# A new written-out plan for a fused attention and mixture-of-experts kernel, with the last results kept in k's buffer and the last narrow store on two queues

## The chip, the cores and the metric

The kernel runs on one core of a Trainium2 chip: TensorE (PE, with its weight loads PEld shown apart), VectorE (DVE), ScalarE (ACT), GpSimd (POOL), and SyncE (SP), which here only issues DMAs. ACT and POOL can issue DMAs too. The metric is the device time of one execution in microseconds (us). The median of 13 runs of the kernel before is 226.5 us, from 225.05 to 229.55.

## The reference

Two layers in a row, for a batch B of 8, 8 heads, a sequence S of 576 and a head size of 64 (a model width D of 512), with 4 experts of width 64, of which each token uses two:

```python
def _attn_ref(q, k, v, g_norm):
    kv = np.einsum('bhsd,bhse->bhde', k, v)
    out = np.einsum('bhsd,bhde->bhse', q, kv)
    rms = np.sqrt(np.mean(out * out, axis=-1, keepdims=True) + 1e-06)
    return (out / rms * g_norm).astype(np.float32)

def _moe_ref(x, w_gate, wq, wk, wv, wo):
    logits = x @ w_gate
    ...
    for e in range(E):
        q = x @ wq[e]; k = x @ wk[e]; v = x @ wv[e]
        scores = scale * (q @ k.transpose(0, 2, 1))
        ...
        ye = a @ v @ wo[e]
        ...
```

The first layer is linear attention without a mask, normalized over each head. In the second, `w` is the softmax over the two best logits of a token, `a` the softmax of the masked scores, and `ye` is added with its `w` where the expert was chosen. The first layer's output, with the heads side by side, is the x of the second layer, which is causal attention inside each expert.

## The kernel before

The sequence is cut into five blocks of tokens, four of 128 and one of 64 (numbers 0 to 4; block 4 is the narrow one). The two layers run batch by batch. For a batch b the steps, with the short names that the plan uses, are:

- Loads: `lk`, `lv` (k and v, in four parts for batch 0 and two for the others), `lkr`, `lvr` (the last 64 tokens of k and v, two DMAs each), `lq` (q; five blocks of two DMAs for batches 0 and 1, eight pieces for the others). The weights come by `lw` and `lwo`, with `ws` (POOL or DVE) and `wo` (ACT) to scale or convert them.
- `kv` 0 to 3: the products of k and v on PE, two heads each, all in one PSUM bank. `kvc` copies them to the tile kvx (line 420). `kgm` and `kgr` multiply them with the gate's weights and sum (lines 425 and 432, DVE); `kgx` copies those sums into kvx as well. For batch 0 these four steps are split in two halves, the second of which needs kv 2.
- `q`, `qc`: q transposed on PE and copied (batches 0 and 1), or transposed by DVE (the rest).
- `out` 0 to 4: q times kvx (line 466); `oc` copies a block to the tile o_sb; `sq`, `red` square and sum it (lines 492 to 502); `ln`, `rs` and the four small steps `na` to `nd` make the reciprocal root; `gl`, `lg` the gate's logits.
- `xm` scales a block (line 557, POOL), `x` transposes it on PE, `xc` copies it to xT.
- `m8`, `sh`, `ex`, `md`, `mk`, `gt`, `den`, `rd`, `gate`: the gate, on [128 x 20] tiles.
- `v`, `qp`, `kp`: the projections on PE, with copies `vc`, `qpc`, `kpc` (tiles vext, qTp, kT).
- `sc`, `exp`, `msk`: scores in four pieces for each of two pairs of experts (line 672, PE; line 686, ACT; line 692, POOL). `pv` (line 706): the products with v in two groups of blocks, 0 to 2 and 3 to 4. `rc`, `iv`, `oc2` (lines 723, 727, 734) divide by the row sums and multiply with the gate. `ot`, `otc` transpose and copy the result to OT.
- `y` (line 764, PE), `yc` (the copy to SBUF, line 771) and `st` (the store, line 777). The narrow block's result lies as two halves of 64 partitions and 256 columns, so its store is two DMAs.

What runs on which engine is not found by a scheduler when the kernel is built: it is written out in four constants. `ORDER` lists all 1291 steps, two characters for each; every engine works through its own in that order. `ENGINE` has a letter for each step that can run on more than one engine: A for ACT, V for DVE, G for POOL. `SLOTS` gives the buffer or PSUM slot that each tile takes when it is first used. `ZEROS` puts matmuls of a zero tile, whose results nothing reads, ahead of some steps of PE.

PSUM is held as four pairs of two banks. The code tracks for each bank which engine used it last; an instruction of another engine on the same bank waits for that one (`own_waits`), also if both only read. So two engines that read one bank take turns.

All loads but batch 0's v are issued on SP's queue, and all stores. Batch 0's `lvr` and `lv` go by ACT's queue. Small loads of the norm's and the gate's weights go by POOL's, at the start. In the built program every load or store on SP's and ACT's queues waits for the one eight before it, counted over both queues in the plan's order.

The results `y` have four SBUF buffers, y0 to y3, in turn; a copy into one waits until the store that last read it is done.

Of the kernel before, what the change touches and what calls it, by code (L numbers as in the profile page):

```python
# [24 lines left out]
ORDER = (
    "090E010403080507020u060H0v003F0D0c0A0F0G3C0b0J0I0d0C0a0j0i0B0e0f0k390s0g3H0l0m0h0t381A0n163B1C1B1D0w3718170o19"
    "0y3A0x1Q0q1R0p0z1S1T3Y0U1U0r0+1V3Z3E1k1E1F1G12100-1H5f1h1I111l143U1m3G1J131Y151i3V3D1K1j1Z1L1M3L1a0S1N1O3K5g0V"
    "3I1P1W3S5l1b1X0K1n3J3T0Q1e3W3M3N0M3Q5i1q1o1r1p3X0T1c5e3O1f1s201g3P225c213q1d0L1+233r3R5d3e0R1-1t3a0N3f1u5b3g3i"  # L30
    "1v3b3h3m3c0W3s3d2W3j5j3t3n243k2X0O3o3l2UAS3p253u1y2V1w5h1z3v3w2e1x3x5r3y2f5m3z2b460X2Y2h885s2c4C5p2i2Z5k0P5q40"
    "4D5t5uAV474E4926485v8C43418D274A5w423+4S4B2d5n3-2E2g4T2H284F2F442a864I4U4G2I4J4H5y2G452B5o292k4V4K2j4L5x4Q2J2C"
    "2A2l802m4M2n4N4a2o4R2D2p2q2r2L0Y4b2KAR2P4Y2M2Q2N2R2O4y4Z854l4z4c4m814i4d4n4f5z4+5+4j844e5-4g4k4-89630Z4h836059"
    "6450615A535156826B6562575B6766525487586C6F68552SAa6D6G2s4O2T2t4W6H8A6E692x4X6A344P2yAZ316I4p35324o2z6J4t8H6K4u"
    "4q4v6L364r8G6M4s6N8N8F6O6d338E8MAX4w8I6X2+4x8B8J6e2-5D6U6f6Y308K2u6R6ZAW6V5H2v6t8L5I6a6W5J6S2w6u5CAT6T6P6r5E5F"
    "6Q6b6s6p6g6cCt6x5G6j6h6q6k6v6i6y8P6l7N6w6m8O7P7OCz6n8UAc6o7QAe8Y8VAU8W7a8Z7X7b7R7Y8Q7c8XAd7S7Z7U8R8g8a7TAY5K7V"
    "8b6-8hAb8S7W8c5L8i708TC-7d8d8j7e8e6z7fCs7i7j8f7gAi6+7hCxAh8k7k8l7A8m77Ao8n7BC+748o7C7871An8pAgCy8yAq72AfAp92Cv"
    "5Y758zAk8-7l5Z93Aj8+5V5a948v5PAl905QFU8q9I915W5R8s8wAm9J9K5X8x7m73Av8r769LCw7995AzAw9896D199977DAx9A8t9BCuA+7F"
    "Ay7GAr8uA-7H9C9QAs9DD0B0AtB59RFM7EAuB17ID3B67J9q7KHjB7DD9OB8B2HkD59rB3D69PD7HiB49bDC9YB99c9VBA9Z9d9SD2D4BB9T9a"
    "9ED8FHBC9oD99WBD9UBE9G9FBFFQDABT9M7L5M7M9HFJBN5S9p5NBU5T9N7wBQBGBV9-5UDB9s7xA09vBK9tBW9y7yDE7q9wBXBOBZDF5OBHBL"  # L40
    "BPBRHlBMBaA1DK9XBS9u9zBj9xDLHm9eBk9+9f7r9gDOFLBYDM9jA2BbDP7sA39k9hFODNBlDQBIFRA7A4BmBc9lDSA8DRA5BJFIBdA9BpBeDT"
    "A69iBnBqFKBhBoCFBiHnDGCGDWFTDHCDDXHqDIDJDYBfHuCEDUDZAA9mBg7nAB9nCQFPDVCNCRCK7oCSCOCHFXFNCICPFW7pFYCLCJFVFSDaCM"
    "ALDbFZDcCTDdFaAMHoCUDeACDfCYDlAFFbANAD7tAGBrDgAECVFcCWDhCZDiCaAHHyCXBsHxHr7uDoHzFeDuC07vDxBwC1FgBzBxHvBtDyFdD+"
    "HwDrB+FfDvHtD-AIH+ByBuFlB-DwAJHpDzC2FtE0H-BvAKC3FuE1FmC4HsFpI0FnFhFqE2FoE3FrFxI1C8C5C9FiC6FsAOFy7zFjAPDsCA7+AQ"
    "C7CbFzDpDtFkCBCc7-DmI3FvDqEAF+CCDjFwE8DkCgF-E9CpG0DnChCmI2CqCiG1EgCnG2I4CrG3G4I5CdG5EhCoEGEBG7CeG6CfGMCjGAEHI6"
    "CkGPGNIAClGQI7GOGJEEIBI8IMEFICECINI9ERGREDGDELIDESEOGSEMEIGTE6IOEJGKGUIEIPGGGLEPEeEKENIFEQE7IIEfIGETE4IHIJErE5"
    "ElIKEsEiEmEoEVEtILEjEUEnEZGEEaEWEbIQEXGBEpEkEYGHEcGFEqG8GIGCGZEdIRG9GbISGaITGXIUGcIVGdGYIWGVIbIXGfGeInIYGWH3Gg"
    "IqIoIrIpIkEvH4EuEzH5IsEwE+ItExE-IeEyIlH6IuF0IvIcImIhF1HGIdH7HHHAH8HIHDFEHEF5H9FFIyFGF6HBHFF8IzFBF9F7HCF2FCIiFA"
    "IZFDIjIfIaGhIgF3IwGiJ0F4IxGsJ1GpGtGjGqGuGmJWGkGrJ6GnJXGlJYGoJ7I+JZJ2I-J4J3GwJ5GvG+HKG-GxH0GyJHGzJaJIHJHOJbJJJj"
    "HPHLJgHQHMJkHNJcJhJBJlJEHRJCJiH1J8HSH2JFJDJdHfJ9JGHWHgHcHhJeJAHZHdJLHaJfHeJKHXJPJmJQHbJMJRJnJNJoHYJOJpJUHTJqJS"  # L50
    "JVJrJuJTJsHUJvJtHVJ-K2K0JwJyJxK1K3K8K4JzK5J+K6K7K9KA"
)
ENGINE = (
    "VAVAVAVAVAVVVVVVVVVVVGVVVVVGVGVVVAVAVVVVAVVVVVVVVAVAVAVAVAVVAVVVAVVAAVVVAVVAAVAAAGAGAAGGAGAAGGAGGVGVVGVVGVVGVV"
    "GVVVGAGGGVVGVVVVVVVVVVVVVVVAGVAGVAGVAGVVVGVVGVVVVAVVVAGVAGVAGVAGVVVGVVGVVAVAVVAVVAVVAVVVVVVVVVVVVVVVVVVVAVVAVV"
    "VAVAVVVVVAAVVAAVVAAVVAAVVAAVAAGGGGGVGVAGVAGVAGVAGVAVGAGGGVVGVAVAVVVVVAVAVVVAGVAGVAGVAGVVVGVVGVVAVVVVVAGVAGVAGV"
    "AGVVVGVVGVVVVAVVAVVAVVVVVAVVVVVVVVVVVVVVVVVVVAVVAVVVVVAGVVVGVVAAVVVGVVAGVAAGGGGGVGVAGVAGVAGVAGVAVGAGGGVVGVVVVV"
    "AVVVAVAVAVAGVAGVAGVAGVVVGVVGVVAVVVVVAGVAGVAGVAGVVVGVVGVVVVVVVAVVAVVVVVAVVVVVVVVVVVVVVVVVVVVVVVVVVVVVAVVAGVVVAV"
    "VAGVVVGVAAGGAGGVGVAGVAGVVGVAGVAVGAGGGVVGVVVVVVVVVVVVVVVAGVAGVAGVAGVVVGVVGVVAVVVVVAGVAGVAGVAGVVVGVVGVVVVAVVAVVV"
    "VVAVVVVVVVVVVVVVVVVVVVVVVAVVAVVVVVVGVVAAVVAGVVVAVVVAVAAAGGGGVGVAGVAGVAGVAGVAVGAGGGVVGVAVAVAVAVAVVVVVAGVAGVAGVA"  # L60
    "GVVVGVVGVVAVAVVVAGVAGVAGVAGVVVGVVGVVAVAVVAVVAVVAVVAVVVVVVVVVVVVVVVVVVVVVVAVVVVVAAVVVGVVVGVVAGVVVAVAAAGAGGVGVVG"
    "VVGVAGVAGVVVGAGGGVVGVVVAVAVVVAVVVVVAGVAGVAGVAGVVVGVVGVVVVVVAVAGVAGVAGVAGVVVGVVGVVVVVVVVVVVVVVVVVVVVVVVVVVVVVVV"
    "VVVVVVVVAVVVVVAGVVVGVVAAVVAGVVAGVAAAGAGGVGVVGVAGVAGVVGVAVGAGGGVVGVVVAVAVVVVVAVAVAGVAGVAGVAGVVVGVVGVVVVVVAVAGVA"
    "GVAGVAGVVVGVVGVVVVAVVAVVAVVVVVVVVVVVVVVVVVVVVVVVVVVVVVVVVVVVGVVAGVVAAVVAGVVAGVAAGGGGGVGVVGVVGVVGVVGVVVGAGGGVVG"
    "VAVVVVVAVVVAVAVAGVAGVAGVAGVVVGVVGVVVVVVVVAVAGVAGVAGVAGVVVGVVGVVVVAVAVVAVVVVVAVVVV"
)
# [52 lines left out]
def kernel(  # L119
# [161 lines left out]
    def copy(task, dst, src):  # L281
        if engine[task] == "A":
            nc.scalar.copy(dst, src)  # L283
        else:
            nc.vector.tensor_copy(out=dst, in_=src)  # L285
# [580 lines left out]
```

The softmax here doesn't subtract the row's maximum and nothing guards it: scores larger than these inputs give would overflow.

## Time and profile before

The profiled execution took 226.79 us; its span, from the first instruction to the last, is 225.08 us, and 1.71 us lie around it.

| Where | What | us |
| --- | --- | --- |
| runs | median of 13 | 226.5 |
| profile | the execution / its span | 226.79 / 225.08 |
| page, 1 | ACT, POOL busy | 133.3, 125.7 |
| order of time | first zero matmul on PE | 1.25 |
| order of time | first `kv` product of batch 0 | 9.92 |
| order of time | first `out` | 18.05 |
| order of time | first `x` | 26.32 |
| order of time | first `v` projection | 35.35 |
| order of time | last `exp` ends | 214.6 |
| order of time | last y copy ends | 221.43 |
| order of time | last store's issue ends | 222.7 |

A row in order of time begins with its start and length, then the engine, the line and operation, the tiles written and read, the form, and in brackets how long the engine had been idle before it and what ended that. The granted clock is that of TensorE, as a share of its full rate. The zero matmuls all lie in the first 14.4 us.

The transfers of the first 125 us keep the 16 DMA engines nearly full; from 158 us on only stores are left. The page's row of it, in tenths for 40 slices:

```profile
DMA  4978979998999987988799999897334000040065
```

### The profile page before, as it was taken

How to read it: one execution, taken by the hardware profiler on the slowest of the kernel's cores; microseconds unless marked ns; L12 is line 12 of the kernel's file. 1: busy time of each engine (PE TensorE's matmuls, PEld its weight loads, DVE VectorE, ACT ScalarE, POOL GpSimd, SP SyncE). 2: the span in 40 equal slices, each digit the busy share in tenths (PEclk: the TensorE clock that was granted, in tenths of full speed). 3: DMA queues.
4: the chain of work that ended last, by engine and by line, in shares of the span. 5: the costliest groups of instructions: out<-in, count | busy, mean ns of one | idle time of the engine just before them, and what ended most of it. 6: DMA issues, size and time to landing. Idle time of an engine off the chain costs nothing. (4 is left out here: it accounts for less than half of the span.)

```text
span 225.1 us, 6608 instructions
## 1 busy us (share of the span) xinstructions
PE 210.5 (94%) x2550; PEld 179.1 (80%) x2562; DVE 157.5 (70%) x366; ACT 133.3 (59%) x265; POOL 125.7 (56%) x278
## 2 busy tenths in 40 slices
...
DMA  4978979998999987988799999897334000040065
GB/s 130 316 223 263 299 183 231 342 230 112 163 326 236 152 191 236 205 164 183 180 229 301 288 231 256 144 227 138 73 106 155 3 0 4 23 186 3 0 216 210
DMA packets 92576, 40.29 MB, mean 179 GB/s; under 512 B 66688, under 2 KB 88192, under 8 KB 92544
## 3 DMA queue, kind: packets, MB, share of 16 engines
...
q0 software_dynamic: 128, 0.01, 0.0%
...
## 5 line engine op out<-in xcount | busy, mean ns | idle before, releaser
L686 ACT ACTIVATE PT<-p 128x1024 bf16<-128x1024 f32 (+1 forms) x64 | 50.3, 841 | 6.6 <-PE p L672 6.1
L692 POOL TENSOR_SCALAR_AFFINE_SELECT PT<-PT 128x256 bf16<-128x256 bf16 (+1 forms) x80 | 29.1, 382 | 26.4 <-ACT PT L686 25.8
L557 POOL TENSOR_TENSOR x_tok<-o_sb,rstd 128x512 fp32r<-128x512 f32 x40 | 43.0, 1130 | 0.5
L466 PE MATMUL p<-kvx,qT 128*128 128x136 f32 (+1 forms) x320 | 39.2, 285 | 1.1 <-DVE kvx L285 0.7
L466 PEld LDWEIGHTS p<-kvx,qT 128*128 128x128 f32 (+1 forms) x320 | 34.7, 179 | 3.9 <-DVE kvx L285 0.9
L502 DVE TENSOR_REDUCE ms<-sq 128x8 f32<-128x520 f32 (+1 forms) x40 | 26.9, 684 | 7.3 <-POOL sq L498 3.6
L498 POOL TENSOR_TENSOR sq<-o_sb 128x512 f32<-128x512 f32 (+1 forms) x20 | 20.6, 1038 | 12.7 <-DVE ms L502 6.4
L626 PE MATMUL p<-wv_r,xT 128*128 128x256 f32 x160 | 25.6, 295 | 0.7 <-ACT xT L283 0.7
L567 PE MATMUL p<-ident_r,x_tok 128*128 128x128 f32 (+1 forms) x160 | 23.4, 279 | 0.7 <-DVE vext L285 0.3
L567 PEld LDWEIGHTS p<-ident_r,x_tok 128*128 128x128 f32 x160 | 20.6, 191 | 3.8 <-POOL x_tok L557 1.0
L672 PE MATMUL p<-qTp,kT 64*128 64x64 f32 (+4 forms) x192 | 22.0, 343 | 1.3 <-DVE kT L285 0.5
L283 ACT COPY o_sb<-p 128x544 f32<-128x544 f32 (+1 forms) x29 | 15.1, 532 | 13.0 <-PE p L466 12.5
L626 PEld LDWEIGHTS p<-wv_r,xT 128*128 128x128 f32 x160 | 21.2, 192 | 1.9 <-ACT xT L283 0.8
L645 PE MATMUL p<-xT,wk_r 128*128 128x288 f32 x128 | 21.0, 307 | 0.0
L405 PE MATMUL p<-v_b,k_b 128*64 128x64 f32 x512 | 20.1, 224 | 0.0
L764 PE MATMUL p<-wo_b,OT 128*128 128x512 bf16 (+1 forms) x85 | 18.2, 343 | 1.7 <-issue 0.5
L645 PE MATMUL p<-xT,wq_r 128*128 128x288 f32 x128 | 19.8, 300 | 0.0
L405 PEld LDWEIGHTS p<-v_b,k_b 128*64 128x64 f32 x512 | 17.8, 138 | 2.3 <-issue 1.9
L672 PEld LDWEIGHTS p<-qTp,kT 64*128 64x128 f32 x192 | 14.2, 185 | 6.4 <-ACT PT L686 1.5
L645 PEld LDWEIGHTS p<-xT,wk_r 128*128 128x128 f32 x128 | 17.8, 190 | 1.5 <-DVE xT L285 0.5
L285 DVE COPY o_sb<-p 128x544 f32<-128x544 f32 (+1 forms) x19 | 12.0, 629 | 9.5 <-PE p L466 4.2
L706 PEld LDWEIGHTS <-PT 128*128 128x128 bf16 x480 | 16.6, 99 | 2.4 <-POOL PT L692 0.5
(111 smaller groups left out, 348.0 us busy)
## 6 DMA issues: line engine op xcount, KB each, us to landing
...
```

Source lines behind the costliest of these rows:

```text
L405: nc.tensor.matmul(p_kv[hh * Dh : (hh + 1) * Dh, c, :], lhsT=lhs, rhs=rhs, start=(j == 0), stop=(j == NF), skip_group_check=True,)
L466: nc.tensor.matmul(p_o[p0 : p0 + nt, c // 2, c % 2 * 256 : c % 2 * 256 + 2 * GW], lhsT=qTs[b % NQT][:, c * S + i * P : c * S + i * P + nt] ...
L498: nc.gpsimd.tensor_tensor(out=dst, in0=src, in1=src, op=AluOpType.mult)
L502: nc.vector.tensor_reduce(mss[b % 2][:nt, i, :], sqs[(NB * b + i) % 3][:nt], axis=AX_X, op=AluOpType.add)
L557: nc.gpsimd.tensor_tensor(out=buf(("x", b, i), [P, NCH, P], FP32R, "x_tok")[:].rearrange("p c (h r) -> p h r c", h=H), in0=ob[:, i, :, 0:D ...
L567: nc.tensor.matmul(p_t[:, c * P : c * P + nt], lhsT=tiles["x", b, i][:, c, :], rhs=ident_r[:, 0:nt], start=True, stop=True)
L626: nc.tensor.matmul(p_v[:, 0 : E * Hd], lhsT=blocks_of(xTs[b % 2], c)[:, i * P : (i + 1) * P], rhs=w_r["v"][:, c, :, :].rearrange("p e f -> ...
L645: nc.tensor.matmul(p_p[:, s, 0:HALF], lhsT=w_r[nm][:, c, 2 * pr : 2 * pr + 2, :].rearrange("p e f -> p (e f)"), rhs=blocks_of(xTs[b % 2], ...
L672: nc.tensor.matmul(p_s[:, el, o : o + hi - lo], lhsT=kTs[(2 * b + pr) % 3][pp, kb * P : (kb + 1) * P], rhs=tiles["qTp", b, pr][pp, lo:hi], ...
L686: nc.scalar.activation(PT[:, :, d0 : d0 + o], big("sc", b, pr, j)[:, :, 0:o], ACTF.Exp, scale=scale)
L692: nc.gpsimd.affine_select(out=d, in_=d, compare_op=AluOpType.is_ge, fill=0.0, base=0, pattern=[[0, 2], [1, w]], channel_multiplier=-1,)
L764: nc.tensor.matmul(p_y[o * nq : (o + 1) * nq, 0:w], lhsT=lhs, rhs=wo_b[:, pr, o * w : (o + 1) * w], start=(pr == 0), stop=(pr == EP - 1), ...
```

## The change

Three things change; nothing of what is computed does.

1. `ORDER`, `ENGINE`, `SLOTS` and `ZEROS` are new. 163 of the steps that can run on either of two engines move to the other one: ACT now has 14 of the 16 kT copies (6 before), 30 of the 40 xT copies (24), 30 of the 40 o_sb copies (24), 22 of the 40 vext copies (17) and 19 of the 40 y copies (25). The zero matmuls become 22 ahead of `gb` (the gate weights' products, now PE's first real step), 3 ahead of q(0,0) and 1 ahead of out(0,4): 26 in place of 22.

PE's order for batch 0, before and after (numbers in brackets: batch and block, or batch and part):

```
before  q(0,4) gb kv(0,2) gr kv(0,1) kv(0,3) kv(0,0) q(0,3) q(0,0) out(0,4) out(0,3) out(0,0)
        q(0,1) q(0,2) q(1,4) out(0,1) out(0,2) x(0,4) q(1,2) x(0,3) x(0,0) kv(1,3) kv(1,2) kv(1,0) ...
after   gb gr q(0,2) kv(0,3) kv(0,1) kv(0,0) q(0,3) q(0,4) kv(0,2) q(0,0) out(0,4) out(0,3) out(0,0)
        out(0,2) q(0,1) q(1,0) q(1,3) out(0,1) q(1,4) q(1,1) x(0,3) x(0,4) x(0,0) v(0,3) v(0,0) v(0,4)
        kv(1,3) kv(1,2) kv(1,0) kv(1,1) x(0,2) x(0,1) q(1,2) ...
```

The loads and stores in their order, the start:

```
before  lvr(0) lq(0,4) lv(0,0) lk(0,2) lv(0,1) lkr(0) lv(0,2) lv(0,3) lk(0,1) lk(0,3) lk(0,0) lq(1,2)
        lq(0,3) lq(0,0) lvr(1) lq(0,2) lq(0,1) lk(1,1) lq(1,4) lv(1,0) lkr(1) lk(1,0) lv(1,1) lw(v,1) ...
after   lvr(0) lk(0,1) lk(0,3) lv(0,0) lq(0,2) lv(0,1) lv(0,2) lv(0,3) lkr(0) lk(0,0) lq(0,3) lq(0,4)
        lk(0,2) lw(q,1) lvr(1) lq(0,0) lv(1,1) lq(1,0) lq(1,1) lq(0,1) lq(1,3) lv(1,0) lw(v,0) lq(1,4)
        lk(1,0) lw(v,1) lk(1,1) lkr(1) ...
```

The `ws` of the first q weights is now POOL's first step of the plan, ahead of two of its memsets. At the end, PE's order differs in a few places, `yc` of blocks 1 and 2 of batch 6 go from ACT to DVE, and in batch 7 ACT gets blocks 0 (of batch 6), 1 and 4, DVE blocks 2, 0 and 3.

2. The last batch's results of blocks 0 to 3 go to one tile in a slot of k's buffers, so they share no buffer with earlier stores.

3. The second half of the last batch's narrow block is stored by ACT's queue; the first half stays on SP's. The last store on SP is now block 3.

```diff
-ZEROS = {("q", 0, 4): 8, ("gb",): 2, ("kv", 0, 2): 6, ("kv", 0, 1): 3, ("q", 0, 3): 3}
+ZEROS = {
+    ("gb",): 22, ("q", 0, 0): 3, ("out", 0, 4): 1,
+}
...
+    def y_t(b, qc):
+        if b == B - 1 and qc < NF:
+            return buf(("k", "y"), [P, NF, D], FP32, "k_b")[:, qc]
+        return buf(("y", b, qc), [P, D], FP32, "y")[:]
+
     def y_copy(b, qc):
         w = D * blocks[qc][1] // P
-        copy(("yc", b, qc), buf(("y", b, qc), [P, D], FP32, "y")[:, 0:w], small("y", b, qc)[:, 0:w])
+        copy(("yc", b, qc), y_t(b, qc)[:, 0:w], small("y", b, qc)[:, 0:w])
 
     def store(b, qc):
         s0, nq = blocks[qc]
         for o in range(P // nq):
             w = D * nq // P
-            nc.sync.dma_start(out[b, s0 : s0 + nq, o * w : (o + 1) * w], tiles["y", b, qc][o * nq : (o + 1) * nq, 0:w])
+            eng = nc.scalar if b == B - 1 and o else nc.sync
+            eng.dma_start(out[b, s0 : s0 + nq, o * w : (o + 1) * w], y_t(b, qc)[o * nq : (o + 1) * nq, 0:w])
```

More of the change, by code (lines that the diff above doesn't have):

```diff
@@ L20 @@
 PARTS = (((0, 1), (1, 3), (3, 5)), ((0, 5),), ((0, 5),), ((0, 5),), ((0, 5),), ((0, 5),), ((0, 5),), ((0, 5),))
-ZEROS = {("q", 0, 4): 8, ("gb",): 2, ("kv", 0, 2): 6, ("kv", 0, 1): 3, ("q", 0, 3): 3}
+ZEROS = {
+    ("gb",): 22, ("q", 0, 0): 3, ("out", 0, 4): 1,
+}
 ORDER = (
[L28 to L51, printed above, removed]
@@ new lines @@
+    "090206010C03050708000H0D0E040M0F3C0q0G0J0d0A0r0I0b0a3A3D0s0f0e0u0g3E0c0N0v0h0j0B0i0k0m3G0t0n0l381A160S1C1B3H1D"
+    "0w181237190y171Q0o1R0U140z1S15393Q1T1E1F1U0x1G3W1V3R1H0p1k1I133B3X0+1J0T5g3Y1h103S0-3Z5c111Y1i3T1K3F1l1L1j0V1Z"
+    "1m1M0O201a1N1O5f1P1w211W221b1x1X0K3L231n0Q3K1e5l3I1q3J1o5e1r1p1f1s3M1t1u1c1v3N1g3U1d5d0P2U3O5b260R2V3P3V3q270L"
+    "3e873r3a5j3f3g3i5o3b3h3m3c3j893k2W3s3d3n5i3l243o2X3t5h5r3p255n2e3u3v2E3w2b2f3x0W5q3y862F2g5s2H3z5p2c8B4C2Y5u2I"
+    "1y465k2Z281z2B5t405m5v2h294D47490Y4E2i2C415w48801+430X4A1-424S3+4B442G3-824T4O4F452A4U4I4P4G4J4a4H5y2d4V4K842D"
@@ new lines @@
+    "4L5x2a4Y2j4b2JAT0Z2L4M5z4N4Z2l2P5+8D2Q4l4c4m2p2K2R4d2q4n882r5-2M2N4e2O638A604i61812k64624f4j2m4y2n2o65AX4k4g4+"
+    "66AS4z4h6B4-6F6CAd596G506D5A53518556676H6E57835B2S6I522s684Q582T542t4WAV694R2x8N4X348C552y6A4p2z356J4o4t6K8M31"
+    "4u6L362+6M4q326N4r2u6O2-5D4v6dAR4s5C5H4w6X5E336e4x8H6f305F6U5G8G8F8P6R8E8O2v6Y5ICt8J6a6V2w6Z6S6P6WAU8I6b6T8K6t"
+    "6c6r6u6p5JAc6s8L6v6Q6q6g8U6wC+6j6h6k6i8Y8V6lCw6m6n8W8Q6o8Z8XAY7N8aAb8R8b7P8S7OAW5K8T7Q8gD25L6-Aa8h8i7aD3707X7R"
+    "7b7Y7U8j7cCy8c7S7ZCz6z8d7T7V8eAZAi6+Ah7W8fAe7A778k7B748lFH787C71Ag7279Af5YCx8mAk75736x8n8o5V5ZC-8p6y5PAj76Al5M"
@@ new lines @@
+    "8y5W5a7D5Q7EAo5N925X8z7F7I5R7eAmAq8+8-935O7iAp7d94D08v9I7fAn909J8q5SD1918s8w8rAv958xCv7j5T967k988t7gAw997h7G9K"
+    "7J8u7HAz5U977KAx9A9L9QCu9BAyA+9CA-9DAr9RB0CsB5AsB1B6AtAuB7FQ7lB29qDD7mB3FTB89E9rDE9OFM9FB49o9PFLDFB9DCBA9bBB9Y"
+    "FJ9cBC9V9p9d9ZD5FUD69W9a9-FOD7BDA09XBE9sA1HqBF9v9tD4BTBGBWHp9y9wD9BN9SBU9THi9GBXDABZBQBOBVD89MBPDB7LBaHjBH9H9N"
+    "BR9z7MBjBKDOBSBkHnBYBl9UDPBbDK9uBcBmFIDQ9xBd9+9eDRDLBLBe9gHrA2DM9h9iA3BMDN9fFKA77qA4A89jA5A97w9k7rA6DS7x9l7sBI"
+    "DTBh7yBJDGBiHkBpDHDIBnHmBqDJCFBoDUFNCDCGHtDVFWCEHlFXCQCNCRCKCSCOFRCHFVCICPFYFPDWCLFaCJAAFSBfDXCM9mFbABHv7nBrFZ"
@@ new lines @@
+    "DY9nHuBgFcALDZBsCTHo7oAMCUDaCVC0DbCWCYBz7pDcC1CXBwCZB+DdCaBtC2FeANDeHyDfBuB-FdHsHxDlFgBxHzFfHwDgACDiDhH+FlDxAD"
+    "H-DoAEAFFm7tAGDyFpFnDzI0AHFhD+FqDuFoI1FrAOFiD-7zDrAPFxFsFjAQCb7+FyE0DvBvFkFtBy7-DwCcFzE17uC3FuC4I37vFvAIF+DsAJ"
+    "I2DpDtAKDmFwEADqDnDjF-E2EBI4E6E3G0DkG1E8C8I5G2C9G3EgE9G4CAG5C5E7G7G6EGEhGMC6GPI6C7GNEHGQGAGOEEI7GRGJGSGTIAEFI8"
+    "IMIBERGDINELESEOEMI9EIICECEJGKEDGGIEIDGLEPGUCBEKIFIIENCCEQIOEeIGIJIPCgEfIKIHCpChCmCqETCiErILElEsCrCnEiIQEtEmEo"
+    "CdCoCjIREjEnCeE4ISITCfGEEpEkGBCkGHGFEqG8GCIUClGIGZIVG9IWGXE5IbIXGaGdGYGbInGeIYGVGcGfGWIqIoIrIpIkH3GgIsIeItEvIu"
@@ L52 @@
+    "H4EVIhEzEuEZEUEwIlEaExEWEbE+IiEXE-IvH5ImIjEyEYF0H6J0F1EcJ1IcEdHGIdH7HHHAH8HIHDFEHEF5H9FFIyFGF6HBHFF8IzFBF9F7F2"
+    "HCFCIZFAIfIaFDGhIgIwF3GiJWF4IxGsJXGpGtGjGuGqGmJ6GkGrJYGnGlJ7I+GoJZJ2I-J4J3GwJ5GvG+HKG-GxH0GyJHGzJaJIHJHOJbJJJj"
+    "HPHLJgHQHMJkHNJcJhJEJlJBHRJFJiJ8HSH1J9JGJdH2HfJCJAHWHgJeHZJDHhHXHcHaJLJfHYJKHdJmHbJMJPJnJNJoJQHeJOJpHTJqJSJRJu"
+    "JTJrJUHUJsJvJtJVJ-HVK2K0JwJyK3K1JxJzK4K8K5J+K9KAK6K7"
 )
 ENGINE = (
-    "VAVAVAVAVAVVVVVVVVVVVGVVVVVGVGVVVAVAVVVVAVVVVVVVVAVAVAVAVAVVAVVVAVVAAVVVAVVAAVAAAGAGAAGGAGAAGGAGGVGVVGVVGVVGVV"
@@ L55 @@
[L55 to L64, printed above, removed]
@@ L65 @@
-    "VAVVVVVAVVVAVAVAGVAGVAGVAGVVVGVVGVVVVVVVVAVAGVAGVAGVAGVVVGVVGVVVVAVAVVAVVVVVAVVVV"
+    "VAVAVAVAVAVVVVVVVVVVVVVGVVVGVVVVVAVAVVVVVVVVVVVVVAVVVAVVVVVVAVVAAVVVAVVVAVVAAVAAGGAGAAGGGGAAAGAGGVGVAGVAGVAGVA"
+    "GVAVGAGGGVVGVAVVVVVAVAVAVAVAGVAGVAGVAGVVVGVVGVVVVVVAVAGVAGVAGVAGVVVGVVGVVVVAVVAVVAVVVVVVVVVVVVVVVVVVVVVVAVVAVA"
+    "VVVVVAVVVAGVVAAVVAAVVAGVVAGVAAAGAGGVGVAGVAGVVGVAGVVVGAGGGVVGVAVVVAVAVAVAVVVAGVAGVAGVAGVVVGVVGVVVVVVAVAGVAGVAGV"
+    "AGVVVGVVGVVAVAVVAVVAVVAVVAVVVVVVVVVVVVVVVVVVVAVVVVVVVVVAVVAAVVAGVVAGVVVGVAAAGAGGVGVAGVVGVAGVAGVVVGAGGGVVGVAVAV"
@@ new lines @@
+    "AVAVVVVVAVAGVAGVAGVAGVVVGVVGVVVVVVAVAGVAGVAGVAGVVVGVVGVVAVVVVAVVVVVAVVVVVVVVVVVVVVVVVVVVVVAVVVVVVVVAGVVAAVVAAV"
+    "VAGVVAGVAAAGGGGVGVAGVAGVAGVAGVAVGAGGGVVGVVVAVAVVVVVAVAVAGVAGVAGVAGVVVGVVGVVVVVVAVAGVAGVAGVAGVVVGVVGVVAVAVVVVVA"
+    "VVAVVAVVVVVVVVVVVVVVVVVVVAVVVVVVVVAAVVAAVVAAVVAGVVVGVAAGGAGGVGVAGVAGVAGVAGVAVGAGGGVVGVVVVVAVVVVVAVAVAGVAGVAGVA"
+    "GVVVGVVGVVAVAVAVAGVAGVAGVAGVVVGVVGVVVVVVVAVVVVVVVVVVVVVVVVVVVVVVVVVVVVAVVVVVVVVAAVVAAVVAAVVVGVVAAVAAGGGGGVGVAG"
+    "VAGVVGVAGVAVGAGGGVVGVAVVVAVAVVVAVAVAGVAGVAGVAGVVVGVVGVVAVAVAVAGVAGVAGVAGVVVGVVGVVAVAVVVVVVVVVVVVVVVVVVVVVVVVVV"
@@ L66 @@
+    "VVVVVAVVAVVVVVVAVVAGVVAAVVAGVVAGVAAGGAGGVGVAGVVGVAGVAGVAVGAGGGVVGVVVVVAVAVAVVVAVAGVAGVAGVAGVVVGVVGVVVVVVVVAGVA"
+    "GVAGVAGVVVGVVGVVVVAVVVVVVVVVVVVVVVVVVVVVVVVVVVVVVVAVVAVVVVVAGVVAGVVVGVVAGVVVAVAAGGAGGVGVVGVVGVVGVAGVVVGAGGGVVG"
+    "VVVVVAVAVVVAVAVAGVAGVAGVAGVVVGVVGVVAVAVVVAVAGVAGVAGVAGVVVGVVGVVVVVVVVVAVVVVVVVVAV"
 )
 SLOTS = (
-    "00001110101112023002102233201400051233020013433023201032531021332240313130230101330223032101201101312231100321"
-    "03213023001450125330041553671046715124206076504703012002312304131301521310305463730144000161154030511021123100"
@@ L70 @@
-    "21032031300212304020355310033454230511002671100030021301312130131233012011162710120630302105741002011007622113"
-    "76237645370022034133033513001020167021101712013140501230131220522000011345101132110062711036712067201230130130"
-    "0130210201126701672451030121067001267145340621"
+    "00000232113011012116270332430526703203146320720300302012030301231025312211310014153101541100212100310103210301"
+    "01013203145674523304500110411567211261010064576213201304101230122220312345364301124503541254101123010131013010"
@@ L73 @@
+    "03110113202331020033304453205672160132012003120013201023060012017014150230121310111030312120434223335002011320"
+    "12131000530432013231026711062140527312001671456201510014250322401310141501101670120673203617223263130203120110"
+    "1010231201322033230011223301100123023167621"
 )
```

## The prediction

> **What bounds the kernel now.** I read the page's busy shares first, then the stretches (busy time by window), then the first 19 us and the last 8 us in order of time.
>
> ```profile
> PE 210.5 (94%) x2550; PEld 179.1 (80%) x2562; DVE 157.5 (70%) x366; ACT 133.3 (59%) x265; POOL 125.7 (56%) x278
> ```
>
> PE is the bound; no other engine passes 70%. The stretches say where PE is not. Their columns are the stretch, its length, then busy time (and instructions) of PE, PEld, DVE, ACT and POOL, the granted clock, the DMA share and GB/s.
>
> ```profile
> 6.06:18.05 11.99, 9.53 (x137) 6.24 (x137) 5.86 (x19) 2.88 (x6) 1.97 (x10) 1.00 0.92 260
> 18.05:26.32 8.27, 7.09 (x81) 6.36 (x81) 3.77 (x7) 5.37 (x16) 2.29 (x6) 1.00 0.98 289
> 26.32:35.35 9.03, 8.87 (x168) 8.30 (x166) 7.01 (x16) 3.92 (x11) 7.33 (x14) 1.00 0.80 200
> 35.35:53.85 18.50, 18.14 (x205) 16.77 (x204) 13.44 (x23) 12.33 (x26) 9.41 (x14) 1.00 1.08 249
> 53.85:57.26 3.41, 2.49 (x21) 1.88 (x20) 2.50 (x10) 2.86 (x8) 2.92 (x11) 1.00 0.84 145
> 57.26:60.68 3.42, 3.42 (x39) 2.97 (x38) 1.98 (x7) 2.62 (x4) 1.59 (x6) 0.50 1.49 147
> 60.68:208.10 147.42, 144.90 (x1759) 127.81 (x1767) 110.95 (x248) 93.26 (x182) 90.13 (x189) 1.00 0.70 163
> 208.10:225.10 17.00, 11.27 (x140) 6.87 (x140) 7.80 (x23) 9.58 (x15) 4.87 (x17) 0.98 0.40 141
> ```
>
> From 60.68 to 208.10 PE idles 2.52 us in 147.42 (1.7%), from 35.35 to 57.26 it idles 1.28 in 21.91 (5.8%), and 57.26 to 60.68 ran at half clock: 3.42 us for 1.71 us of work. So a new order can win at most 3.8 us of idling plus 1.7 us of clock in the middle; the rest lies in the first 35 us and the last 17.
>
> In the start the load queue and a chain on DVE decide:
>
> ```profile
> 4.82 2.49 SPq L306 DMA_DIRECT2D k_b<-in_k_dram  x3
> 13.66 0.69 DVE L425 TENSOR_TENSOR kvg<-p,wg_t 128x512 f32<-128x512 f32 x1 [0.74 <-PE p L405]
> 15.51 0.69 DVE L425 TENSOR_TENSOR kvg<-p,wg_t 128x512 f32<-128x512 f32 x1 [0.66 <-ACT kvx L283]
> 16.12 1.27 DVE L432 TENSOR_REDUCE kvxg<-kvg 128x8 f32<-128x512 f32 x2
> 17.30 0.69 DVE L285 COPY kvx<-kvxg 64x8 f32<-64x8 f32 x4
> 18.05 2.73 PE L466 MATMUL p<-kvx,qT 128*64 128x136 f32 x24 [0.70 <-DVE kvx L285]
> ```
>
> The first out matmul waits for kvx, the last of a chain behind the four kv products; the second kvg multiply waits for ACT to leave the same bank. That is a turn of readers.
>
> **The start, step by step.** In the program's order every load waits for the one issued eight loads before it; SP, free at 4.23, issues its next k load at 4.82. Landings of before in the first 20 us, issue to landing: k_b 5.2 us (3.7 to 5.6), q_b 4.1 to 4.7, v_b 4.5 to 5.5, v_rem 2.8 to 3.6. One SP issue takes some 0.63 (six q loads in 3.80).
>
> The 22 zero matmuls ahead of gb start at 1.25 as before. The eight of before go 0.43 apart up to 4.21; the two at 13.75 take 0.59. With the fast pace from 6.06 on, 11 go slow and 11 at 0.22 (half of 0.43) to 0.30: done by 8.5 to 9.4. gb took 1.9 (7.29 to 9.2), gr 0.55, block 2's q transposes 0.87, three kv products 1.75: 13.6 to 14.5, where all four kv ended at 13.5 before. DVE then does the first half's chain (multiply 0.69, two copies 0.58, sum 0.64, a q copy 0.42, two copies 0.34) until 16.4 to 17.3. I take the early end, under which the zeros are covered by the load below; the late one costs 0.9.
>
> kv(0,2) is now the last product, and its k load stands behind lk 1, lk 3, lq 2, lkr, lk 0, lq 3 and lq 4. Counted with ACT's six, it is the 18th load and waits for the tenth, ACT's last v load (issued 5.0, landing 5.5 later). It goes at 10.3 to 10.5 and lands near 15.6; kv(0,2) ends at 16.2. Behind it on DVE, from 16.4: the second half's 0.69, 0.58, 0.64, a q copy of 0.68 put between, 0.34. Out begins at 19.3: 1.25 later than 18.05.
>
> What follows makes it up. Behind the first four outs (3.5 us: 22.8) come q(0,1), q(1,0), q(1,3), out(0,1), q(1,4) and q(1,1), together 4.9. lq(0,1) is the 29th and 30th load; those eight before it land at some 17.2, it goes by 18.9 and lands at 23.1, so this ends at 28.0. The chain from out to x (squares, sums, ln, exp, the Newton steps, xm at 1.10) takes 8.0 by the same rows; before it took 8.3 (18.05 to 26.32). So x begins at 28.0, x(0,0) waits for the third xm until 29.3, and three v (1.65) and four kv(1) (2.4) end at 34.0; the loads of batch 1 land by 31 (the last, the 41st, waits for the 33rd, which lands at 25.7, and takes 5 more). By 34.0 PE has done two x and one q less and three v more than before at 35.35, net 0.3 less waiting: before was there at 35.05. **Gain 1.0.** Bounds: with out at 18.05 still, 2.1; the other end is the last rival's loss of 2.8.
>
> POOL's weight product, moved to its head, holds its queue until a load near 16.5; the next product on POOL is needed after 24.
>
> **The middle.** All matmuls, exps and masks remain. Of the copies, ACT gets some 13 us more (8 kT casts at 0.64, 6 o_sb at 0.61, 6 xT at 0.60, 5 vext at 0.37, less 6 y at 0.60 and some small ones): 133 becomes 146, DVE falls by 15. Neither is near PE. What the turns taken into account are worth is not to be read off the rows, so by bounds: all 3.8 us of idling gone, or the 5.8% of 35.35 to 57.26 everywhere: 9.9 instead of 3.8 us in 169.3, a loss of 6.1. I take the early stretch coming down to the 1.7% of the later one: 1.28 to 0.37, **gain 0.9**, because its idling follows single copies (0.54 behind a kT copy, 0.38 behind xT), which is what turns order.
>
> The clock: half rate came after a stretch with PE busy 2.49 of 3.41 us; but 12.89 to 16.30, busy 2.36 of 3.41, was followed by full rate. So the rows give no threshold: it may go (gain 1.7), stay, or one more come, likeliest at 19.7, behind the start's wait for lk 2 (loss 1.7). I take **0.4**, a little weight on going.
>
> The Trainium skill, "TensorE: Matmul & The Clock Gate", Part 1, says that the rate halves after at least one idle window of about 3.4 us. This trace disagrees: 73% busy was enough once. By the page no plan here would be halved at all, and the slow stretch of before would go: 1.7 in place of 0.4.
>
> **The end.** ACT's last eight exps and PE's sequence are nearly the same.
>
> ```profile
> 219.55 0.95 PE L764 MATMUL p<-wo_b,OT 128*64 128x256 bf16 x6 [0.46 <-ACT OT L283]
> 220.58 0.59 ACT L283 COPY y<-p 128x512 f32<-128x512 f32 x1 [0.59 <-PE p L764]
> 221.01 0.42 DVE L285 COPY y<-p 128x256 f32<-128x256 f32 x1 [1.68 <-DMA out_dram<-y]
> ```
>
> The last y copy waited 1.68 for a store to leave its buffer; with the results in k's buffer, read last by kv near 154, that wait goes. But behind it lies ACT's copy to 221.17, so no more than 0.26 is free. Then two issues on SP (the second at 222.1, landing 2.1 later) become one of 256 KB behind the last copy, landing in 2.5; the narrow block's second half goes by ACT, whose queue has nothing behind it. Against that, two y copies of batch 6 go from ACT, which idles 1.53 behind them, to DVE, ahead of the reciprocals: three at 0.64 (two took 1.28 at 195.75) from 213.4 end at 215.3; the first reciprocal ran at 214.85. That is 0.45 later down the chain osc, ot, y, so the last copy ends near 221.6, its store goes at 221.7 and lands at 224.2, as before. **Sum of the end: 0**, bounds 0.6 less and 0.8 more.
>
> **Sum.** The profiled execution took 226.79, its span 225.08 and 1.71 around it. 1.0 + 0.9 + 0.4 + 0 = 2.3 less gives 224.5. That execution lies 0.3 above the median, so 224.2 against 226.5.
>
> **The rivals.**
> - *More of the same*: no half clock (1.7), half of the idling (1.9), start 1.0: 4.6 less, 221.9. For it: the copies behind single idles; against: the later 147 us are at 1.7% already.
> - *The loads hide it*: the DMA share is 1.08 from 35.35 to 53.85, and the same bytes must land before kv of batch 2 (kv(2,2) at 46.8). If that landing sets PE's pace, the start's gain is waited away, and only 0.2 to 0.4 of idling moves: 226.2. Against: PE waited for a DMA only 0.7 us in all of before.
> - *The loads come late* (the slower side): lq(0,1) stands 1.0 MB further back, and half-megabyte loads land in 6.2 (k_b's median over the whole run), not 4.7. Three turns of eight then bring batch 1's kv loads to 31 + 3 x 1.5 = 35.5, PE waits at 31.7 for 3.8: start 1.0 gained becomes 2.8 lost, 229.3. It decides from 32.7 on. For it: PE has only four zero matmuls left there; against: DMA moved 260 to 289 GB/s, enough for these bytes by 30.
> - *New places cost elsewhere*: idling at 4% of the middle, between 1.7 and 5.8: 6.8 in place of 3.8, less the start's 1.0: 228.5. For it: 163 copies and small steps change their engine; against: nothing but PE is near its limit.
>
> **Chances.** Forecast (222.8 to 225.4) 0.44, more of the same 0.12, hidden 0.18, loads late 0.14, idling elsewhere 0.12. Half a per cent is 1.1 us, about what a measurement can tell: faster 0.56, same 0.18, slower 0.26. The forecast's own range is 222.8 to 225.4; 8 in 10 needs all but the ends of the rivals: 221.5 to 228.8.
>
> **What would show it.** Out's first matmul at 19 to 20.2; kv(1) done by 34; PE idle from 35 to 208 below 3 us; no row at half clock inside the span; the last copy of y by DVE near 221.6 less the gain. It is wrong if PE stands before a batch-1 load past 32.7, or if a half-clock stretch appears near 20, or if the idling in the middle is 6 us.

## The result and the profile after

The changed kernel took 230.54 us (median of 11 runs, 228.11 to 231.57) against 226.58 for the kernel before beside it: ratio 1.0161, 95% interval 1.013 to 1.0192. It is slower, and lies outside the range that was predicted. The ratios, here and below, leave out each kernel's slow runs (over 1.5% above its fastest); by them the change costs 1.6%, some 3.6 us, where the medians differ by 4.0. The profiled execution took 231.57, the longest of these runs, with a span of 229.86: 4.78 more than before's 225.08.

The page of the changed kernel, busy shares and the granted clock in 40 slices:

```profile
PE 214.3 (93%) x2554; PEld 182.1 (79%) x2566; DVE 151.8 (66%) x346; ACT 146.0 (64%) x288; POOL 123.1 (54%) x275
...
PEclk9999999999799999999999979999999999999997
```

ACT's 146.0 is what the prediction counted, and no engine but PE is near its limit. The clock row (tenths of the full rate) has two dents besides that of the last slice, at slices 11 and 24, where before had one, at slice 11. The stretches of the changed kernel (stretch, length, then busy us and instructions of PE, PEld, DVE, ACT, POOL, the granted clock, DMA share, GB/s):

```profile
40.00:57.20 17.20, 15.98 (x190) 14.39 (x185) 10.62 (x18) 14.57 (x28) 12.27 (x17) 0.99 1.09 179
57.20:60.61 3.41, 3.41 (x17) 3.29 (x17) 1.55 (x8) 2.48 (x7) 1.73 (x7) 0.54 0.86 251
60.61:107.00 46.39, 45.98 (x624) 39.66 (x625) 31.88 (x69) 32.69 (x63) 26.93 (x58) 1.00 0.98 197
107.00:128.87 21.87, 20.64 (x227) 18.39 (x226) 17.36 (x41) 16.16 (x32) 12.40 (x30) 1.00 0.93 211
128.87:132.28 3.41, 1.33 (x13) 1.12 (x12) 3.34 (x4) 2.51 (x6) 3.11 (x6) 0.96 1.41 148
132.28:135.70 3.42, 3.39 (x16) 3.40 (x17) 0.43 (x2) 1.14 (x2) 0.92 (x3) 0.54 1.12 317
135.70:215.00 79.30, 77.53 (x934) 68.91 (x940) 52.75 (x124) 55.40 (x109) 44.40 (x100) 1.00 0.44 108
```

These windows begin some 0.3 us behind the clock's own slow stretches, which lie at 56.89 to 60.30 and 131.99 to 135.40; so their rows show 0.54 and not 0.50. From 60.61 to 107 PE idles 0.41 us in 46; from 107 to 132.28 it idles 3.31 in 25.28. In the stretch at 128.87 PE works 1.33 us of 3.41, DVE 3.34, in only four instructions. Here they are in order of time, with the sum ahead of them, then the rows of POOL and of PE (changed kernel):

```profile
127.37 1.22 DVE L434 TENSOR_REDUCE kvxg<-kvg 128x16 f32<-128x1024 f32 x1
128.62 2.82 DVE L287 COPY kvx<-kvxg 64x16 f32<-64x16 f32 x2
131.47 0.42 DVE L287 CAST vext<-p 64x256 bf16<-64x256 f32 x1
131.81 0.44 DVE L287 COPY OT<-p 128x576 bf16<-128x576 bf16 x1
```

```profile
127.59 1.12 POOL L559 TENSOR_TENSOR x_tok<-o_sb,rstd 128x512 fp32r<-128x512 f32 x1
128.59 0.25 POOL L605 TENSOR_SCALAR g_mk<-g_mk 128x20 f32<-128x20 f32 x1
128.82 2.08 POOL L559 TENSOR_TENSOR x_tok<-o_sb,rstd 128x512 fp32r<-128x512 f32 x2
130.82 0.41 POOL L694 TENSOR_SCALAR_AFFINE_SELECT PT<-PT 128x256 bf16<-128x256 bf16 x1
...
131.53 0.23 POOL L608 TENSOR_TENSOR g_gt<-g_ex,g_mk 128x20 f32<-128x20 f32 x1 [0.30 <-ACT g_ex L595]
```

```profile
129.50 0.69 PE L628 MATMUL p<-wv_r,xT 128*128 128x256 f32 x4
132.31 1.05 PE L468 MATMUL p<-kvx,qT 128*128 128x136 f32 x3 [2.11 <-DVE OT L287]
```

Two copies of 64 x 16 elements (`kgx`: the gate's sums into kvx) take 2.82 us together. The first lies there from 128.62 to 131.25 and ends 0.03 after POOL stops being busy without a break; the second takes 0.17. Behind them on DVE stand the copies of vext and of OT, and PE's out(5) waits 2.11 us for that last one. In the kernel before these copies ran on ACT in batches 2, 4 and 5; the new `ENGINE` has them on DVE in batches 2 to 5. (Batch 3 had them on DVE before too.)

Where the 4.78 us went: up to the point of equal work that the prediction set (35.05 before) 0.28, since kv(1) ends at 35.33; from there to the last exp (214.58 before, 219.46 after) 4.60, of which PE's idling 2.70 (4.21 to 6.91) and its busy time 1.90, which holds the second half-clock stretch; behind the last exp 0.10 less.

### The profile page after: what moved, and what is told of

Same layout as the page of the kernel before. It is cut to its first block, busy times and chain, and to the rows that moved or that the text cites. A ratio compares the mean times of both kernels' runs of the same rounds, so it can differ in the third digit from the quotient of the medians.

```text
span 229.9 us, 6604 instructions
## 1 busy us (share of the span) xinstructions
PE 214.3 (93%) x2554; PEld 182.1 (79%) x2566; DVE 151.8 (66%) x346; ACT 146.0 (64%) x288; POOL 123.1 (54%) x275
## 5 line engine op out<-in xcount | busy, mean ns | idle before, releaser
L468 PE MATMUL p<-kvx,qT 128*128 128x136 f32 (+1 forms) x320 | 40.9, 290 | 4.0 <-DVE OT L287 2.1
L468 PEld LDWEIGHTS p<-kvx,qT 128*128 128x128 f32 (+1 forms) x320 | 36.2, 183 | 7.0 <-DVE OT L287 2.3
L628 PE MATMUL p<-wv_r,xT 128*128 128x256 f32 x160 | 27.3, 305 | 1.7 <-DVE xT L287 0.8
L500 POOL TENSOR_TENSOR sq<-o_sb 128x512 f32<-128x512 f32 (+1 forms) x19 | 19.5, 1038 | 15.0 <-ACT o_sb L285 7.2
L628 PEld LDWEIGHTS p<-wv_r,xT 128*128 128x128 f32 x160 | 22.2, 199 | 4.1 <-ACT xT L285 1.5
L285 ACT COPY o_sb<-p 128x544 f32<-128x544 f32 (+1 forms) x35 | 19.0, 544 | 7.7 <-PE p L468 7.2
L285 ACT CAST xT<-p 128x512 fp32r<-128x512 f32 (+1 forms) x30 | 16.2, 554 | 10.6 <-PE p L569 6.9
L647 PE MATMUL p<-xT,wk_r 128*128 128x288 f32 x128 | 20.5, 305 | 0.0
L458 DVE STREAM_TRANSPOSE qT<-q_b 128x576 f32<-128x576 f32 x24 | 17.7, 752 | 0.9 <-DMA q_b<-in_q_dram 0.6
L647 PEld LDWEIGHTS p<-xT,wq_r 128*128 128x128 f32 x128 | 17.5, 188 | 0.7 <-issue 0.2
```

The source lines that it names most:

```text
L468: nc.tensor.matmul(p_o[p0 : p0 + nt, c // 2, c % 2 * 256 : c % 2 * 256 + 2 * GW], lhsT=qTs[b % NQT][:, c * S + i * P : c * S + i * P + nt] ...
L628: nc.tensor.matmul(p_v[:, 0 : E * Hd], lhsT=blocks_of(xTs[b % 2], c)[:, i * P : (i + 1) * P], rhs=w_r["v"][:, c, :, :].rearrange("p e f -> ...
L647: nc.tensor.matmul(p_p[:, s, 0:HALF], lhsT=w_r[nm][:, c, 2 * pr : 2 * pr + 2, :].rearrange("p e f -> p (e f)"), rhs=blocks_of(xTs[b % 2], ...
```

## The experiments

The theory, after this reading, is a collision: a copy on DVE from SBUF to SBUF stands still while POOL works there. Its rivals are that the new order and its loads cost the time, that only the half clock does, and that the end does.

**e1, the copies back on ACT.** In the changed kernel:

```diff
     engine = dict(zip(ns, ENGINE))
+    engine.update({("kgx", b, 0): "A" for b in (2, 3, 4, 5)})
```

> The changed kernel with one edit: the copies of the gate sums into kvx (kgx) of batches 2 to 5 run on ACT (before: ACT in 2, 4, 5; changed: DVE in all four). The theory (collision): on DVE these copies of fp32 from SBUF to SBUF, 0.16 us alone, stood still while POOL ran xm (lasting 1.85, 1.63 and 2.82 us for two in batches 2, 4 and 5), and out(4) and out(5) and their followers waited. Then all six copies take 0.2 on ACT, DVE's stretched operations sum to under 1.5 us instead of 6.3, PE's idling from 40 to 215 us falls from 6.7 to 3.5-4.5, and the time from 230.5 to 226-228; the lower end if the second half-clock stretch at 132 goes with the gap at 130. Rival (the new order and its loads cost it, the copies only fill time that is waited for anyway): 229.5 to 230.5 still. Rival (only the half-clock stretch matters): 228.8.

Measured: 226.66 us (226.13 to 227.44, 12 runs), 1.0029 of before (0.9994 to 1.0063), so 3.9 below the changed kernel by the medians, and 1.3% (some 3.0 us) by the ratios. PE idles 2.86 us from 40 to 215 instead of 6.73, less than the 3.5 that was expected. The same two stretches as above in this kernel:

```profile
128.87:132.28 3.41, 3.04 (x49) 2.95 (x49) 1.61 (x6) 3.21 (x8) 2.23 (x8) 1.00 1.10 281
132.28:135.70 3.42, 3.42 (x53) 3.04 (x50) 3.03 (x9) 1.58 (x4) 0.51 (x3) 1.00 1.10 258
```

The gap and the half clock behind it are gone, with order, loads and zeros as they were; so is the half-clock stretch at 57. The rivals that blame the order and its loads, or the half clock alone (228.8), fall.

**e5, another operation at the same place.** The copies stay on DVE, in the same order, but each is a sum over an axis of one element:

```diff
-            copy(("kgx", b, g), kvx[b % 2][pp, cs, hh, Dh:GW], kvxg[b % 2][pp, cs])
+            dst, src = kvx[b % 2][pp, cs, hh, Dh:GW], kvxg[b % 2][pp, cs]
+            if engine["kgx", b, g] == "A":
+                nc.scalar.copy(dst, src)
+            else:
+                nc.vector.tensor_reduce(dst, src.unsqueeze(3), axis=AX_X, op=AluOpType.add)
```

> The changed kernel with kgx left on DVE, but as a sum over an axis of one element instead of a copy; nothing else moves. It asks what about the copy collides with POOL. If it is the copy's own mode (the sums of kvg, fp32 in SBUF too, ran at 1.21 beside POOL's xm without stretching): each takes 0.15-0.25 in all batches, PE idling 40-215 3.5-4.5, time 226-228 as with ACT. Rival (any DVE operation that reads and writes SBUF waits for xm, or SBUF's bandwidth is short): the same 0.6 to 2.6 us pairs, 230.5.

Measured: 225.61 us (224.45 to 229.39), 0.995 of before (0.9913 to 0.9987). The profiled execution was the longest of the twelve, 229.39, and PE idles 3.90 us in it from 40 to 215; what is read from it here are single operations. In this profile the pair of batch 5 runs amid the same operations of POOL (DVE, then POOL):

```profile
129.97 0.34 DVE L446 TENSOR_REDUCE kvx<-kvxg 64x16 f32<-64x16 f32 x2
```

```profile
128.94 1.11 POOL L563 TENSOR_TENSOR x_tok<-o_sb,rstd 128x512 fp32r<-128x512 f32 x1
129.94 0.25 POOL L609 TENSOR_SCALAR g_mk<-g_mk 128x20 f32<-128x20 f32 x1
130.17 2.10 POOL L563 TENSOR_TENSOR x_tok<-o_sb,rstd 128x512 fp32r<-128x512 f32 x2
```

0.34 for two, where the copies took 2.82. All eight copies of this form (busy us, mean ns), first the changed kernel, then this one:

```profile
L287 DVE COPY kvx<-kvxg 64x16 f32<-64x16 f32 x8 | 6.6, 823 | 0.1
```

```profile
L446 DVE TENSOR_REDUCE kvx<-kvxg 64x16 f32<-64x16 f32 x8 | 1.2, 155 | 0.1
```

So it isn't DVE's load, nor its place in the order, nor SBUF in general: it is the copy. The Trainium skill, "SBUF — State Buffer", section "Who interferes with whom", says this: copies on DVE can run in a mode that takes a second pair of ports, shared with GpSimd; who issues first holds it for its whole instruction and the other stands still; a reduce never takes that pair. The runs agree, 823 against 155 ns; that it is the ports is the page's account, and no run here shows the ports themselves. The wait can be longer than one instruction: the copy of 128.62 was passed over while POOL finished five operations in a row.

**e2 and e7, the same move in the kernel before.**

```diff
+    engine.update({("kgx", b, 0): "V" for b in (2, 4, 5)})
```

> The kernel before with one edit: kgx of batches 2, 4 and 5 on DVE, as in the changed kernel. Collision: POOL's xm runs at 105.8-106.9 and 122.7-126.8 where DVE would be free for these copies (105.5 and 124.1), so the pair of batch 4 takes some 1.4 and that of batch 5 some 2.7 instead of 0.33; that of batch 2 meets no xm (POOL has done the fifth at 53.3, DVE free at 53.7) and stays at 0.33. The time: 226.6 plus 0.5 to 2.5, thus 227 to 229. Rival (new order and loads): 226.4 to 226.8, no stretched copies.

Measured: 228.41 us (226.72 to 229.91), 1.0082 of before (1.0041 to 1.0122), 1.85 more. The pairs took 1.49 and 1.18 in batches 4 and 5 (1.4 and 2.7 were expected), and 0.34 in batch 2, at 55.35, where POOL stood idle. The profile, of one of the shorter runs (227.21), shows PE idling 4.41 from 40 to 215 against 3.85 before, so only part of the 1.85 is seen in it. With the reduce in their place:

```diff
+    engine.update({("kgx", b, 0): "V" for b in (2, 4, 5)})
...
+                nc.vector.tensor_reduce(dst, src.unsqueeze(3), axis=AX_X, op=AluOpType.add)
```

> The kernel before with the copies of the gate sums (kgx) of batches 2, 4 and 5 on DVE, as in e2, but as sums over one element. In e2 the move alone cost 1.85 us, with pairs of 1.4 and 1.1 us. If the stretching is the cost and not the place on DVE: pairs of some 0.3-0.4 us and a time within 0.6 of before (ratio 0.997 to 1.003). Rival (DVE has no room at these places): ratio 1.006 to 1.010 as e2.

Measured: 226.12 us, 0.9986 of before (0.9949 to 1.0022). The interval lies below that of e2, so DVE has room at these places, and what cost the 1.85 was the standing still. Each copy of 0.4 us or more in these two traces ends just behind an operation of POOL (worked out from starts and lengths):

```
kernel   batch  copy, from - to   took   POOL operation that ended, at
changed    2     53.65 -  54.12   0.47   xm             54.10
changed    2     54.14 -  55.50   1.37   gl             55.47
changed    4    106.12 - 106.76   0.64   xm            106.73
changed    4    106.77 - 107.75   0.98   xm            107.73
changed    5    128.62 - 131.25   2.63   msk           131.22
e2         4    104.98 - 106.11   1.13   msk           106.08
e2         5    125.78 - 126.78   1.00   xm            126.75
changed    3     86.21 -  86.37   0.16   none running
```

**e12, one collision alone.** The changed kernel with the reduce in batch 5 only:

```diff
+            elif b == 5:
+                nc.vector.tensor_reduce(dst, src.unsqueeze(3), axis=AX_X, op=AluOpType.add)
+            else:
+                nc.vector.tensor_copy(out=dst, in_=src)
```

> The changed kernel with kgx as a reduce for batch 5 alone; batches 2 and 4 keep their copies on DVE (1.85 and 1.63 us a pair). If the 2.11 us of idling at 130.2 and the half-clock stretch behind it come from batch 5's pair: no half-clock stretch after 120 in the profile, granted clock of every run above 0.985, and 1.9 to 3.5 us below the changed kernel's 230.5, thus 227.0 to 228.6, still above e5 by the idling of batches 2 and 4 (some 1.3 to 2.0). Rival (any one collision alone is waited away): under 1.0 less.

Measured: 227.01 us (225.84 to 229.57), 1.0022 of before (0.9976 to 1.0067): 3.5 below the changed kernel, where the reduce in all batches, run beside it (226.10, e13 below), is 4.4 below. So most of the loss comes from batch 5. No half clock behind 120, and the granted clock is 0.988 or more in every run. (Its profile has another half-clock stretch, at 17.70 to 21.11.) The stretch that PE had filled to 1.33 us, in this kernel:

```profile
128.87:132.28 3.41, 3.41 (x39) 3.26 (x37) 1.31 (x5) 3.13 (x7) 3.11 (x9) 1.00 0.92 97
```

What batches 2 and 4 still cost (pairs of 1.48 and 1.33 in this profile) seems less than expected: PE idles 2.57 from 40 to 215, and the time is 0.9 above the reduce's 226.10, not 1.3 to 2.0. The intervals are too wide to tell 0.9 from nothing.

**e3 and e10, the zeros.** 17 ahead of `gb` instead of 22:

```diff
-    ("gb",): 22, ("q", 0, 0): 3, ("out", 0, 4): 1,
+    ("gb",): 17, ("q", 0, 0): 3, ("out", 0, 4): 1,
```

> The changed kernel with 17 zero matmuls ahead of gb instead of 22. In the changed kernel the 22 ended at 8.34 and gb began at 8.28 without idling, and every step of PE up to kv(0,2) followed without a wait. If the zeros set the start: gb at 7.0-7.3 (in the kernel before it began at 7.29, so its row of weights was there by then), first out at 18.5-18.9 instead of 19.34, time 0.4 to 0.8 less (229.7-230.1). Rival (the load of kv(0,2)'s k part, issued 10.7, sets it): first out still at 19.2-19.4, time within 0.2.

Measured: 229.35 us (227.97 to 233.0, 6 runs), 1.0104 of before (1.0039 to 1.0168), too wide to tell it from the changed kernel. Its trace tells more:

```profile
7.11 0.64 PE L367 MATMUL p<-kvg,ones 128*64 128x512 f32 x1
...
15.40 0.69 PE L407 MATMUL p<-v_b,k_b 128*64 128x64 f32 x16 [1.65 <-DMA k_b<-in_k_dram]
...
19.26 3.66 PE L468 MATMUL p<-kvx,qT 128*64 128x136 f32 x32
```

`gb` begins 1.17 earlier than the changed kernel's 8.28, but kv(0,2) then waits 1.65 for its load, and the first out comes at 19.26 instead of 19.34. The zeros lie under that load. The same on top of the reduce:

> e5 (the sums as a reduce of one element) with 17 zero matmuls ahead of gb instead of 22. In e3 five fewer moved gb by 1.2 us and the first out by 0.08, as PE then stood 1.65 us for kv(0,2)'s load. If the loads set the start: within 0.4 of e5's run beside it. Rival (the zeros do): 0.6 to 1.2 below it, as first outs were seen at 19.9 and 20.2 where the 22 zeros went slower.

Measured: 226.55 us, 0.9984 (0.994 to 1.0027), and 226.10 for the reduce with 22 zeros beside it: no gain. In this profile kv(0,2) ran at 14.14 without a wait, and PE stood 1.70 for the load of q(0,0) instead; the first out came at 19.08.

**e8, that load earlier.** On top of the reduce and the 17 zeros:

```diff
+    order.remove(("lk", 0, 2))
+    order.insert(order.index(("lq", 0, 3)), ("lk", 0, 2))
```

> The changed kernel with kgx as sums (e5), 17 zero matmuls ahead of gb, and the load of k's part for kv(0,2) issued ahead of q(0,3) and q(0,4) instead of behind them. In e3 PE stood 1.65 us for this load (kv(0,2) at 15.40) and the first out stayed at 19.26. If that load gates the start: kv(0,2) at 13.7-14.2, first out at 18.0-18.4, time 0.5 to 1.1 below e5's 225.6, thus 224.5 to 225.1. Rival (what is gained there is waited for at q(0,0)'s load, at the copies to qT ahead of out(0,1), or at the loads of batch 1): first out before 18.6 but x or kv(1) no earlier, 225.4 to 225.8.

Measured: 226.73 us (224.75 to 229.48), 1.0003 of before (0.996 to 1.0046). The time is neither of the two forecasts, and no gain shows. As the rival has it, x comes no earlier: the first out is at 18.87 (not before 18.6), but q(0,0) waits 0.58 and 0.48 for its own load, q(1,4) 0.72, and x begins at 29.60, where it was 29.07 in e10, the same kernel without this move. There kv(0,2) had run at 14.14, against 14.33 here: in these two executions its load wasn't the gate, and others were waited for.

**e6 and e9, the end.** Parts 2 and 3 of the change in the kernel before, its plan kept:

```diff
+    def y_t(b, qc):
+        if b == B - 1 and qc < NF:
+            place(("y", b, qc))
+            slot_of["k", "y"] = 1
+            return buf(("k", "y"), [P, NF, D], FP32, "k_b")[:, qc]
...
+            eng = nc.scalar if b == B - 1 and o else nc.sync
```

> The kernel before, plan unchanged, with parts 2 and 3 of the change alone: the last results in k's buffer, and the second half of the last narrow store on ACT's queue. The last y copy no longer waits 1.68 us for a store, but ACT's copy of block 3 ends at 221.17 anyway and the last store behind it sets the end. Theory (the end is worth nothing): 0 to 0.4 less than before, ratio 0.998 to 1.000. Rival (the wait and the two issues on SP were on the path): 0.6 or more less, ratio 0.997 or lower. If the end is what costs the changed kernel its time: slower than before.

Measured: 225.93 us, 0.9998 of before (0.9956 to 1.004); behind the last exp lie 10.11 us instead of 10.50. The interval also holds the rival's 0.997, so the runs alone don't decide; the profile is with the theory. And the reverse, the reduce with the old end (the buffers of the last results are set by hand in it, and the narrow block shares one with block 1 of its batch):

```diff
-        if b == B - 1 and qc < NF:
-            return buf(("k", "y"), [P, NF, D], FP32, "k_b")[:, qc]
...
-            eng = nc.scalar if b == B - 1 and o else nc.sync
```

> The changed kernel with kgx as sums (e5), with parts 2 and 3 undone: the last batch's results in the y buffers in turn, every store on SP. Theory (the end is worth nothing beside the rest): 0 to 0.6 above e5, thus 225.6 to 226.2. Rival (parts 2 and 3 carry the gain of e5 over before): 226.4 or more.

Measured: 227.15 us (225.43 to 230.28), 1.0029 of before (0.9988 to 1.007). Behind the last exp lie 11.82 us, 1.41 more than in the reduce's own profile (10.41). Its last y copy, and that of the changed kernel:

```profile
220.17 0.37 ACT L285 COPY y<-p 128x256 f32<-128x256 f32 x1 [2.20 <-DMA out_dram<-y]
```

```profile
225.53 0.37 ACT L285 COPY y<-p 128x256 f32<-128x256 f32 x1 [1.28 <-PE p L766]
```

The time is in the rival's range, 226.4 or more, and not in the theory's. In the new plan, with these buffers, the copy stands for a store; parts 2 and 3 take that away. Against the old plan's end this comes to nothing, 10.40 in the changed kernel against 10.50.

**e13 and e11, does a version beat both?** The reduce once more, and the kernel before with the reduce and parts 2 and 3:

> e5 once more, beside the three others: 0.995 of before again (0.992 to 0.999) if the gain of e5 is real; 1.000 or more if it was the spread of the runs. PE idling 40 to 215 us of 2.5 to 3.5, no stretched copy.

> The kernel before with parts 2 and 3 of the change and kgx of batches 2, 4, 5 on DVE as a reduce of one element. e6 (parts 2 and 3) left 10.11 us behind the last exp instead of 10.50; e7 (the reduce) was at 0.9986 of before. If both add: 0.995 to 0.998 of before. If the new plan is what makes e5 fast, this stays above e5's run beside it by 0.5 or more; if the plans are equal without the collision, within 0.5 of it.

Measured: the reduce 226.10 us, 0.9987 (0.9946 to 1.0028); the old plan with both 225.56 us, 0.9962 (0.9921 to 1.0003). The reduce's two results are 0.995 and 0.9987, so a gain of some 0.3% over the kernel before is likely and not shown. The old plan with both is 0.54 below the reduce, by intervals that overlap: without the collision the two plans can't be told apart.

## Why the prediction was wrong

**The step that failed** is the one on engines in "The middle": "ACT gets some 13 us more ... DVE falls by 15. Neither is near PE." The moves were counted as time added to an engine with room. That 0.16 us copies would become 0.47 to 2.63 on the other engine, for what POOL does meanwhile, was no term at all. The runs showed 2.70 us more of PE's idling and one more half-clock stretch in its place, and 3.0 to 3.9 us that go with the copies alone (e1). In the trace of before the four copies of this form on DVE ran at 169 ns, none of them begun beside an xm, so it shows no stretched one. DVE's busy time fell by 5.7 (157.5 to 151.8) and not by 15; with the copies on ACT it was 145.3. The rival "new places cost elsewhere" had the size (4% of the middle idle; 3.8% came, 6.73 of 175) and the source ("163 copies and small steps change their engine"), and was put at 0.12 because "nothing but PE is near its limit". Its 228.5 was still 2.0 short, as it priced the idling alone and kept the start's gain. Room on an engine said nothing about whom it waits for.

**The middle's gain of 0.9** was taken from "single copies ... which is what turns order". With the copies on ACT PE idles 2.86 us from 40 to 215 against 3.85 before, 1.0 less, so a gain of this size may be there. But single profiles spread: the reduce had 3.90 and 3.15, the old plan with parts 2 and 3 3.68, with the reduce as well 2.81. No time here shows the gain.

**The clock, 0.4:** one more half-clock stretch came instead, but at 132 behind the 2.11 gap, not near 20. (In e12's profile one did come near 20, as the prediction feared.) In runs of the changed kernel with a granted clock of 0.994 or more the time was 228.1 to 229.5, with 0.98 to 0.99 229.0 to 231.6; with the copies on ACT all twelve runs had 0.994 or more. The stretch at 132 was a follower of the collision.

**The start, 1.0 gained,** was mis-sized: 0.28 lost. The steps up to the first out were right: zeros done at 8.34 (just ahead of 8.5 to 9.4), second multiply at 16.33 (16.4), out at 19.34 (19.3), and the zeros were covered by the load, as e3 shows. What followed was put at 4.9 us of products and a short wait for a load, from 22.8 to 28.0; PE took 22.93 to 29.19 for it, 0.85 of that waiting for DVE's copy of qT ahead of out(0,1) and 5.4 in the products themselves. kv(1) ended at 35.33 instead of 34.0. No load of batch 1 was waited for there, so "the loads come late" wasn't it.

**The end, 0:** right, 0.10 less, and partly by luck: with the old buffers, as e9 sets them, the new plan's end was 1.41 longer, a larger term than any in the sum.

With the terms as measured the profiled execution comes out: 226.79 + 0.28 (start) + 2.70 (idling) + 1.90 (busy time, half clock in it) - 0.10 (end) = 231.57.
